# Products of an FFN block summed in any order and far behind the hidden layer, and a second attention transposed by VectorE in 32x32 squares

## The chip, the cores and the metric

The program runs on one core of one Trainium2 chip. Its time is the device time of one launch in microseconds; before the change it is 1913.87 us, the median of three runs (1910.66 to 1913.94).

Five engines work side by side, each through its own instructions in a fixed order: TensorE (PE in the profile; its weight loads stand apart as PEld), VectorE (DVE), ScalarE (ACT), GpSimd (POOL) and SyncE (SP). SP and POOL issue the transfers here. An instruction waits for the semaphores of those it needs, and all that stands behind it on its engine waits with it.

## The reference

Two parts follow each other: an attention through 32 inducing points (the matrix `inducing`, 32x128) on four batches of 12480 rows of 128, and then a feed-forward layer with a squared ReLU on all 49920 rows.

```python
def mab(q, kv):
    s = scale * (q @ kv.transpose(0, 2, 1))
    s = s - s.max(-1, keepdims=True)
    a = np.exp(s)
    a /= a.sum(-1, keepdims=True) + 1e-09
    return a @ kv
h = mab(I, x)                       # 32 x 128 for each batch
x = mab(x, h).reshape(B * S, D)     # 49920 x 128
h = np.maximum(x @ w_in, 0.0)       # 49920 x 2048
out = (h * h) @ w_out               # 49920 x 128
```

## The kernel before

**Units.** A batch is cut into 13 units of 960 rows, so there are 52 units. The *first attention* (class `First`, the inducing points ask all rows) of the units of the next batch runs beside the main work, one unit for each unit; the *second attention* (class `Second`, the rows ask the 32 results) of the next unit likewise. At the end of a batch's first attention, `first_end` joins the sums, and multiplies the joined result with `w_in` once per batch (tile `hw`). So the hidden layer of a unit is one product of the second attention's weights (tile `st`) with `hw`.

**An FFN block** (`ffn_block`) is half a unit, 480 rows. It has four *quads* of four slices of 128 hidden columns. For each quad: two pairs of products `h <- st, hw` (line 782), each pair into one of two PSUM buffers; a Relu by ACT for each pair into one of four tiles `g` (line 790); one Square by ACT for the quad (line 801); a rounded copy `hi` (line 808 by DVE for quads 0 and 2, line 806 by a casting transfer that POOL issues for quads 1 and 3; three buffers); the rest `lo = g - hi` by DVE (line 812; two buffers); and twelve products into the output sum `op` (line 825): four of `hi` with `wo_hi`, four of `hi` with `wo_lo`, four of `lo` with `wo_hi`. They are added to the plan in pairs, and each pair needs the pair before it (`last`), so within a block they stand in one fixed order. The block's sum is transposed by DVE (`rows`, line 840) and stored by four transfers of SP (line 844).

**The second attention** of a unit: scores in four groups of 32 partitions (line 626, `na <- xt, hT`); a copy out of PSUM by DVE (`ss`); two transposes by PE (line 644, `s2t`); maximum, subtraction, Exp by ACT (line 658), sum, reciprocal and share (lines 651 to 672); split into a rounded part and the rest (`sk`, lines 676 and 680); four products with the identity that turn it back (line 687, `ap`); a copy out by ACT or DVE (`sw`); and four transfers of SP (line 702) that spread it into `st`, where each half unit has the weights of its 480 rows in four bands of 32 partitions.

**What sets the order.** `Plan` is a list scheduler that runs before the program is emitted. Each task has an engine, a duration in ns, needs, buffers and a due time. Of the tasks that can start on an engine (within 40 ns of its being free) the one with the earliest due time goes first. The plan's order is the order of the instructions on each engine. Units are due every `PERIOD` = 32000 ns; a block's products are due 8000 ns after its quad's hidden layer, the second attention from `NARROW` = 6000 ns after the unit's start. `narrow` puts the second attention's scores, the first attention's scores (line 430) and its sums (line 484, `nb`) into one task; that task needs `begun`, the first hidden product of the unit that runs.

Of the kernel before, what the change touches and what calls it, by code (L numbers as in the profile page):

```python
# [154 lines left out]
def induced_attention_then_squared_relu_ffn(  # L155
# [17 lines left out]
    NQ = NF // 4  # L173
    GB, HB, LB = 4, 3, 2
# [31 lines left out]
    identr = const.tile([P, P], F32R, name="identr")  # L206
    nc.vector.tensor_copy(identr, ident)

# [408 lines left out]
    class Second:  # L617
# [6 lines left out]
        def score(self, where):  # L624
            for q in range(Q):
                nc.tensor.matmul(  # L626
                    where[q * M:(q + 1) * M, :].rearrange("m (k t) -> m k t", k=2), self.s["hT"][:, :M],
                    self.s["xt"][self.u].rearrange("c (k q t) -> c q k t", k=2, q=Q)[:, q],
                    start=True, stop=True,
                )  # L630

        def weigh(self, scored, where, bank_, due, step):
            v = {}
            n, s, u = self.n, self.s, self.u
            G = 2 * Q

            def evict():
                v["ss"] = att.tile([P, 2 * TS], F32, tag="ss", name=f"ss_{n}")
                copy(te, v["ss"], where())

            def turn():
                v["tp"] = tp = bank(f"s2t_{n}")
                for k in range(2):
                    nc.tensor.transpose(  # L644
                        tp[:TS, k * P:(k + 1) * P], v["ss"][:, k * TS:(k + 1) * TS], ident
                    )

            def top():
                v["tv"] = v["tp"][:TS, :2 * P].rearrange("t (g m) -> t g m", m=M)
                v["mx"] = tiny.tile([TS, G, 1], F32, tag="mx2", name=f"mx2_{n}")  # L650
                nc.vector.tensor_reduce(v["mx"], v["tv"], axis=AX.X, op=ALU.max)  # L651

            def sub():
                v["d"] = att.tile([TS, G, M], F32, tag="d", name=f"d_{n}")
                nc.vector.tensor_sub(v["d"], v["tv"], v["mx"].broadcast_to([TS, G, M]))  # L655

# [3 lines left out]
            def total():  # L660
                v["z"] = tiny.tile([TS, G, 1], F32, tag="z2", name=f"z2_{n}")
                nc.vector.tensor_reduce(v["z"], v["d"], axis=AX.X, op=ALU.add)  # L662
# [4 lines left out]
            def invert():  # L667
                v["rz"] = tiny.tile([TS, G, 1], F32, tag="rz2", name=f"rz2_{n}")
                nc.vector.reciprocal(v["rz"], v["z"])

            def share():
                nc.vector.tensor_mul(v["d"], v["d"], v["rz"].broadcast_to([TS, G, M]))

            def high():
                v["sk"] = att.tile([TS, Q, 2, 2, M], F32R, tag="sk", name=f"sk_{n}", bufs=1)
                nc.vector.tensor_copy(v["sk"][:, :, :, 0, :], v["d"].rearrange("t (k q) m -> t q k m", q=Q))

            def low():
                sk = v["sk"]
                nc.vector.tensor_sub(  # L680
                    sk[:, :, :, 1, :], v["d"].rearrange("t (k q) m -> t q k m", q=Q), sk[:, :, :, 0, :]
                )

            def back():
                v["ap"] = ap = bank(f"ap_{n}")
                for q in range(Q):
                    nc.tensor.matmul(  # L687
                        ap[:, q * TS:(q + 1) * TS],
                        v["sk"][:, q].rearrange("t k a m -> t (k a m)"),
                        identr[:TS, :TS], start=(q == 0), stop=(q == Q - 1), skip_group_check=True,  # L690
                    )

            def stacked():

                v["sw"] = att.tile([P, BLK], F32R, tag="sw", name=f"sw_{n}")
                copy(ts, v["sw"], v["ap"][:, :BLK])

            def spread():
                st = att.tile([P, 2, BLK], F32R, tag="st", name=f"st_{n}")
                for k in range(2):  # L700
                    for j in range(2):
                        nc.sync.dma_start(
                            st[j * 64:(j + 1) * 64, k, :].bitcast(F32),
                            v["sw"][k * 64:(k + 1) * 64, :].bitcast(F32),
                        )
                s["st", u] = st

            bt, ba, bw = Buffer("m"), Buffer("m"), Buffer("sw")
# [4 lines left out]
            t = add("DVE", 340, top, d + step, [t], reads=[bt])  # L713
            td = add("DVE", 340, sub, d + step, [t], reads=[bt])
# [5 lines left out]
            th = add("DVE", 210, high, d + 4 * step, [t], port=True)  # L720
            tl = add("DVE", 335, low, d + 5 * step, [th], port=True)
# [4 lines left out]
    def narrow(second, f, g, due, step, begun=None):  # L726
# [4 lines left out]
        needs = [begun]  # L731
# [7 lines left out]
        def go():  # L739
            if bank_a:  # L740
                v["a"] = bank(f"na_{second.n if second else f.n}")
            if second:
                second.score(v["a"][:, :2 * TS])
            if f:
                f.score(v["a"][:, 2 * TS:4 * TS])
# [7 lines left out]
        if f:  # L753
            f.weigh(t, lambda: v["a"][:, 2 * TS:4 * TS], bank_a, due)
# [168 lines left out]
```

## Time and profile before

| | |
|---|---|
| median of three runs | 1913.87 us |
| the profiled execution's own time | 1910.1 us |
| its span, first to last instruction | 1908.3 us |
| mean granted clock of TensorE | 0.986 of full speed |
| PE busy | 1710.5 us (90%) |
| ACT busy | 1590.1 us (83%) |
| DVE busy | 1462.8 us (77%) |
| POOL busy | 128.9 us (7%) |

Matmuls overlap each other: the mean of one (390 ns) is its latency, and eight in a row take far less than eight times that. So a busy PE is no measure of the work it has left; how often weight loads start in an unbroken row tells more. The names of tiles are the program's without their numbers; `h` and `op` are the two halves of the feed-forward layer.

### The profile page before, as it was taken

The numbers are of one execution on the slowest core, as the hardware profiler recorded it, in microseconds if no ns is written. First come the engines' busy times: TensorE is split into PE (matmuls) and PEld (weight loads), VectorE is DVE, ScalarE is ACT, GpSimd is POOL, SyncE is SP. The second block draws the span as 40 slices with busy tenths as digits, with TensorE's granted clock in tenths as the row PEclk, the third lists the DMA queues.
The fourth block names the chain that finished last, engine by engine and source line by source line (L and its number), as shares of the span: only waits on it lengthen the run. The fifth ranks groups of instructions, "written<-read, shape, count | busy, mean of one in ns | idle before, by whom it ended". The sixth has DMA issues, their size and how long they took to land.

```text
span 1908.3 us, 24030 instructions
## 1 busy us (share of the span) xinstructions
PE 1710.5 (90%) x8897; PEld 1342.1 (70%) x8897; DVE 1462.8 (77%) x1548; ACT 1590.1 (83%) x1602; POOL 128.9 (7%) x230
## 2 busy tenths in 40 slices
PE   7698989889998998989998989899999999998997
PEld 4377767777777777777777767777777777776776
DVE  6677777777887777878787778777777877777776
ACT  5578888788888888888888888888888888888886
POOL 1200000000000000000000000000000000000000
PEclk9799999999999999999999999999999999999999
DMA  9656756666666757667747657667444544444453
GB/s 216 121 156 159 179 159 164 174 159 165 168 165 165 177 163 179 162 173 167 190 141 171 157 170 184 163 164 178 145 140 130 161 148 153 134 152 147 141 159 120
DMA packets 458736, 306.12 MB, mean 160 GB/s; under 512 B 366172, under 2 KB 431484, under 8 KB 458620
## 3 DMA queue, kind: packets, MB, share of 16 engines
q1 hardware_dynamic: 428668, 100.11, 30.7%
q0 software_dynamic: 29952, 204.49, 29.6%
q8 instruction: 70, 1.15, 0.3%
q14 instruction: 46, 0.38, 0.1%
HBM read 48.94 MB, written 25.56 MB: 39 GB/s over the span
## 4 chain that ended last, share of the span: by engine, by line
PE 37%; ACT 21%; issue 15%; DVE 14%; DMA 11%; SPq 2%; DVEq 0%; ACTq 0%; POOLq 0%; POOL 0%
PE op L825 27%; ACT g L790 12%; DVE lo L812 7%; ACT g L801 7%; PE h L782 7%; DMA hi<-g 6%; DVE hi L808 3%; DMA xq<-in_x_dram 3%; SPq L397 1%; DMA words_i<-in_moe_w_in_dram 1%; DVE xt L401 1%; PE wp L586 1%; PE na L626 1%; DVE d L655 1%; ACT d L658 1%
## 5 line engine op out<-in xcount | busy, mean ns | idle before, releaser
L790 ACT ACTIVATE g<-h 128x960 f32<-128x960 f32 x832 | 769.5, 970 | 178.1 <-PE h L782 171.3
L812 DVE TENSOR_TENSOR lo<-g,hi 128x1920 fp32r<-128x1920 f32 x416 | 882.4, 2153 | 36.9 <-DMA hi<-g 28.8
L801 ACT ACTIVATE g<-g 128x1920 f32<-128x1920 f32 x416 | 752.7, 1809 | 5.7
L782 PE MATMUL h<-st,hw 128*128 128x480 f32 x1664 | 481.7, 393 | 104.3 <-ACT g L790 100.0
L825 PE MATMUL op<-hi,wo_hi 128*128 128x480 f32 x1664 | 452.4, 392 | 27.4 <-DMA hi<-g 25.3
L825 PE MATMUL op<-lo,wo_hi 128*128 128x480 f32 x1664 | 429.5, 385 | 17.9 <-DVE lo L812 17.5
L782 PEld LDWEIGHTS h<-st,hw 128*128 128x128 f32 x1664 | 298.4, 189 | 201.1 <-ACT g L790 159.0
L825 PE MATMUL op<-hi,wo_lo 128*128 128x480 f32 x1664 | 429.6, 383 | 0.0
L808 DVE CAST hi<-g 128x1920 fp32r<-128x1920 f32 x208 | 240.8, 1158 | 227.5 <-ACT g L801 226.1
L825 PEld LDWEIGHTS op<-hi,wo_hi 128*128 128x128 f32 x1664 | 303.6, 190 | 103.4 <-DMA hi<-g 41.7
L825 PEld LDWEIGHTS op<-lo,wo_hi 128*128 128x128 f32 x1664 | 305.7, 188 | 81.9 <-DVE lo L812 37.3
L825 PEld LDWEIGHTS op<-hi,wo_lo 128*128 128x128 f32 x1664 | 315.9, 190 | 51.6 <-issue 1.4
L806 POOL DMA_DIRECT2D hi<-g x208 | 110.6, 532 | 1701.6 <-ACT g L801 1366.3
L840 DVE STREAM_TRANSPOSE rows<-op 128x480 f32<-128x480 f32 x104 | 70.7, 679 | 82.6 <-PE op L825 82.6
L658 ACT ACTIVATE d<-d 120x256 f32<-120x256 f32 x52 | 21.7, 417 | 55.4 <-DVE d L655 55.4
L687 PEld LDWEIGHTS ap<-identr,sk 120*128 120x128 f32 x208 | 28.3, 190 | 37.5 <-DVE sk L680 30.6
L687 PE MATMUL ap<-identr,sk 120*128 120x120 f32 x208 | 32.6, 279 | 21.5 <-DVE sk L680 21.2
L401 DVE STREAM_TRANSPOSE xt<-xq 128x960 f32<-128x960 f32 x39 | 45.8, 1174 | 3.9 <-PE na L626 3.8
L651 DVE TENSOR_REDUCE mx<-s2t 120x8 f32<-120x256 f32 x52 | 21.8, 419 | 20.2 <-PE s2t L644 20.0
L662 DVE TENSOR_REDUCE z<-d 120x8 f32<-120x256 f32 x52 | 20.8, 401 | 17.0 <-ACT d L658 17.0
L235 ACT COPY et<-ep 120x256 f32<-120x256 f32 x52 | 19.4, 374 | 16.7 <-PE ep L464 16.0
L626 PE MATMUL na<-xt,hT 128*32 128x240 f32 x416 | 32.7, 387 | 0.0
(91 smaller groups left out, 611.1 us busy)
## 6 DMA issues: line engine op xcount, KB each, us to landing
hi<-g POOLq DMA_DIRECT2D x208, 960.0 KB, 4.1
xn<-in_x_dram SPq DMA_DIRECT2D x52, 480.0 KB, 5.2
st<-sw SPq DMA_DIRECT2D x208, 120.0 KB, 2.3
out_dram<-rows SPq DMA_DIRECT2D x416, 60.0 KB, 2.0
xq<-in_x_dram SPq DMA_DIRECT2D x156, 120.0 KB, 4.4
words_i<-in_moe_w_in_dram SPq DMA_DIRECT2D x4, 512.0 KB, 9.2
words_o<-in_moe_w_out_dram SPq DMA_DIRECT2D x4, 512.0 KB, 7.5
ind_sb<-in_inducing_dram SPq DMA_DIRECT2D x1, 16.0 KB, 1.7
```

What stands on the lines that cost most here:

```text
L401: nc.vector.transpose(self.xt, v["xq"].rearrange("p g c -> p (g c)"))
L626: nc.tensor.matmul(where[q * M:(q + 1) * M, :].rearrange("m (k t) -> m k t", k=2), self.s["hT"][:, :M], self.s["xt"][self.u].rearrange("c ...
L658: nc.scalar.activation(v["d"], v["d"], AF.Exp, scale=scale)
L687: nc.tensor.matmul(ap[:, q * TS:(q + 1) * TS], v["sk"][:, q].rearrange("t k a m -> t (k a m)"), identr[:TS, :TS], start=(q == 0), stop=(q ...
L782: nc.tensor.matmul(c["hp"][:, l, :BLK], s["hw"][:, f * P:(f + 1) * P], s["st", u][:, k, :], start=True, stop=True,)
L790: nc.scalar.activation(v["g"][:, 2 * i:2 * i + 2, :], c["hp"][:, :, :BLK], AF.Relu)
L801: nc.scalar.activation(v["g"], v["g"], AF.Square)
L806: nc.gpsimd.dma_start(v["hi"], v["g"])
L808: nc.vector.tensor_copy(v["hi"], v["g"])
L812: nc.vector.tensor_sub(v["lo"], v["g"], v["hi"])
L825: nc.tensor.matmul(w["op"][:, :BLK], wo[:, 4 * j + l, :], v[name][:, l, :], start=(j == m == l == 0), stop=(j == NQ - 1 and m == 2 and l = ...
L840: nc.vector.transpose(w["rows"].rearrange("p g c -> p (g c)"), w["op"][:, :BLK])
```

## The change

The products of a block no longer form a chain: each pair needs only its input and the block's first pair, so the plan may put them in any order, and they are due 18000 ns after their quad instead of 8000. The scores of a unit's second attention no longer need `begun`, but the spread (`ready`) of the unit two before. In the second attention, the scores are laid out so that each group of 32 partitions holds 240 rows of the unit and 16 more that belong to another group (width 256, a multiple of 32); DVE transposes 32x32 squares straight out of PSUM, the softmax runs as before on 128 partitions, DVE transposes back, splits in two, and sixteen transfers of 32 partitions by 240 columns spread it. The two PE transposes, the four turning products, their two PSUM banks and both copies out of PSUM are gone.

```diff
+    LANE, WIDE = UNIT // Q, 256
+    LANES = [[(0, q * LANE, WIDE)] for q in range(Q - 1)] + [[(0, UNIT - LANE, LANE), (LANE, 0, WIDE - LANE)]]
...
         def score(self, where):
             for q in range(Q):
-                nc.tensor.matmul(
-                    where[q * M:(q + 1) * M, :].rearrange("m (k t) -> m k t", k=2), self.s["hT"][:, :M],
-                    self.s["xt"][self.u].rearrange("c (k q t) -> c q k t", k=2, q=Q)[:, q],
-                    start=True, stop=True,
-                )
+                for to, from_, n in LANES[q]:
+                    nc.tensor.matmul(
+                        where[q * M:(q + 1) * M, to:to + n], self.s["hT"][:, :M],
+                        self.s["xt"][self.u][:, from_:from_ + n], start=True, stop=True,
+                    )
...
             def turn():
-                v["tp"] = tp = bank(f"s2t_{n}")
...
+                v["d"] = tile_of("d")
+                nc.vector.transpose(v["d"].rearrange("p g m -> p (g m)"), where())
...
+            def back():
+                v["a"] = tile_of("a")
+                nc.vector.transpose(v["a"].rearrange("p g m -> p (g m)"), v["d"].rearrange("p g m -> p (g m)"))
...
             def spread():
                 st = att.tile([P, 2, BLK], F32R, tag="st", name=f"st_{n}")
-                for k in range(2):
+                flat = st.rearrange("p k t -> p (k t)")
+                for q in range(Q):
                     for j in range(2):
-                        nc.sync.dma_start(
-                            st[j * 64:(j + 1) * 64, k, :].bitcast(F32),
-                            v["sw"][k * 64:(k + 1) * 64, :].bitcast(F32),
-                        )
+                        for a in range(2):
+                            nc.sync.dma_start(
+                                flat[(2 * j + a) * M:(2 * j + a + 1) * M, q * LANE:(q + 1) * LANE].bitcast(F32),
+                                v["sw"][q * M:(q + 1) * M, a, :LANE].bitcast(F32),
+                            )
...
-            te = add("DVE", 317, evict, d, [scored], reads=[bank_])
-            t = add("PE", 150, turn, d + step, [te], takes=[bt])
...
+            t = add("DVE", 335, turn, d, [scored], reads=[bank_])
...
-            t = add("PE", 460, back, d + 5 * step, [tl], takes=[ba])
-            ts = add(ST, (455, 565), stacked, d + 6 * step, [t], takes=[bw], reads=[ba])
-            self.ready = add("SP", 1000, spread, d + 7 * step, [ts], takes=[self.bst], reads=[bw])
+            t = add("DVE", 335, back, d + 4 * step, [t])
+            th = add("DVE", 210, high, d + 5 * step, [t], port=True, takes=[bw])
+            tl = add("DVE", 340, low, d + 5 * step, [th], port=True, reads=[bw])
+            self.ready = add("SP", 7000, spread, d + 6 * step, [tl], takes=[self.bst], reads=[bw])
...
-                                start=(j == m == l == 0), stop=(j == NQ - 1 and m == 2 and l == 3),
+                                start=len(done) == 1, stop=len(done) == 3 * NF,
...
-                    last = add("PE", 438, products, due + 8000 + 600 * (2 * m + i), [from_, last, w_outs[j]],
-                               takes=[bo] if begin else [], reads=[buf] + ([] if begin else [bo]))
+                    sums.append(add(
+                        "PE", 438, products, due + 18000 + 600 * (2 * m + i), [from_, w_outs[j]] + sums[:1],
+                        takes=[bo] if begin else [], reads=[buf] + ([] if begin else [bo]),
+                    ))
...
-        t = add("DVE", 570, rows, end + 1500, [last], reads=[bo], late=LATE_OT, takes=[br])
+        t = add("DVE", 570, rows, end + 1500, sums, reads=[bo], late=LATE_OT, takes=[br])
...
+        before = seconds[w - 1].ready if w else None
...
-            narrow(seconds[w + 1], f, g, t_u + NARROW, STEP, begun)
+            narrow(seconds[w + 1], f, g, t_u + NARROW, STEP, before)
```

The order on PE where the first block of unit 8 of the second batch begins, before (`h_8_0_1` is the second pair of that block, `op_7_1` the sum of the block before it, `hi_7_1_2` that block's third quad):

```order
L782 MATMUL h_8_0_0_7211<-st_8_7106,hw_4569 128x480 x2
L626 MATMUL na_9_7214<-xt_9_3067,hT_4567 32x240 x4
L430 MATMUL na_9_7214<-xt_9_6974,indT 32x240 x4
L484 MATMUL nb_8_7223<-xn_8_6345,et_8_7040 32x128 x8
L825 MATMUL op_7_1_7157<-hi_7_1_1_7179,wo_hi 128x480 x4
L825 MATMUL op_7_1_7157<-hi_7_1_1_7179,wo_lo 128x480 x4
L782 MATMUL h_8_0_1_7251<-st_8_7106,hw_4569 128x480 x2
L782 MATMUL h_8_0_2_7254<-st_8_7106,hw_4569 128x480 x2
L825 MATMUL op_7_1_7157<-lo_7_1_1_7243,wo_hi 128x480 x4
L825 MATMUL op_7_1_7157<-hi_7_1_2_7208,wo_hi 128x480 x4
L825 MATMUL op_7_1_7157<-hi_7_1_2_7208,wo_lo 128x480 x4
L825 MATMUL op_7_1_7157<-lo_7_1_2_7232,wo_hi 128x480 x4
```

The same place after the change:

```order
L764 MATMUL h_8_0_0_7360<-st_8_7247,hw_4625 128x480 x2
L764 MATMUL h_8_0_1_7363<-st_8_7247,hw_4625 128x480 x2
L807 MATMUL op_7_1_7310<-hi_7_1_1_7291,wo_lo 128x480 x2
L807 MATMUL op_7_1_7310<-lo_7_1_1_7344,wo_hi 128x480 x2
L764 MATMUL h_8_0_2_7375<-st_8_7247,hw_4625 128x480 x2
L807 MATMUL op_7_1_7310<-lo_7_1_1_7344,wo_hi 128x480 x2
L807 MATMUL op_7_1_7310<-hi_7_1_2_7334,wo_hi 128x480 x2
L764 MATMUL h_8_0_3_7386<-st_8_7247,hw_4625 128x480 x2
L807 MATMUL op_7_1_7310<-hi_7_1_2_7334,wo_hi 128x480 x2
L764 MATMUL h_8_0_4_7395<-st_8_7247,hw_4625 128x480 x2
L807 MATMUL op_7_1_7310<-hi_7_1_2_7334,wo_lo 128x480 x4
L807 MATMUL op_7_1_7310<-lo_7_1_2_7365,wo_hi 128x480 x4
```

Between `h_8_0_0` and `h_8_0_3` before there are 24 products of the sum in groups of four, and `h_8_0_3` stands behind all of quad 2; after, there are 8 between `h_8_0_0` and `h_8_0_3`, in groups of two between single pairs of `h`, and `h_8_0_4` stands ahead of eight of quad 2's twelve.

The second attention of unit 8 on DVE, before, from the maximum (`mx_1_8`, read from the PSUM bank `s2t_8` that PE has transposed) to the split (`sk_8`); `hi`, `lo` and `rows` are the feed-forward layer's:

```order
L651 TENSOR_REDUCE mx_1_8_7029<-s2t_8_7006 120x8
L812 TENSOR_TENSOR lo_7_0_0_7034<-g_7_0_0_6936,hi_7_0_0_7001 128x1920
L655 TENSOR_TENSOR d_8_7050<-s2t_8_7006,mx_1_8_7029 120x256
L840 STREAM_TRANSPOSE rows_6_1_7052<-op_6_1_6859 128x480
L662 TENSOR_REDUCE z_1_8_7061<-d_8_7050 120x8
L665 TENSOR_SCALAR z_1_8_7061<-z_1_8_7061 120x8
L669 RECIPROCAL rz_1_8_7076<-z_1_8_7061 120x8
L672 TENSOR_TENSOR d_8_7050<-d_8_7050,rz_1_8_7076 120x256
L676 CAST sk_8_7080<-d_8_7050 120x8x32
L680 TENSOR_TENSOR sk_8_7080<-d_8_7050,sk_8_7080 120x8x32
L808 CAST hi_7_0_2_7085<-g_7_0_2_7019 128x1920
```

After the change, from the sum's safe form (`z_1_8`) to the split (`sw_8`); `a_8` is the second transpose, and the first one (`d_8<-na_8`) stands where the copy `ss_8` stood, behind the scores:

```order
L657 TENSOR_SCALAR z_1_8_7142<-z_1_8_7142 128x8
L661 RECIPROCAL rz_1_8_7158<-z_1_8_7142 128x8
L789 CAST hi_7_0_2_7162<-g_7_0_2_7097 128x1920
L664 TENSOR_TENSOR d_8_7045<-d_8_7045,rz_1_8_7158 128x256
L793 TENSOR_TENSOR lo_7_0_2_7192<-g_7_0_2_7097,hi_7_0_2_7162 128x1920
L793 TENSOR_TENSOR lo_7_0_1_7204<-g_7_0_1_7047,hi_7_0_1_7121 128x1920
L668 STREAM_TRANSPOSE a_8_7216<-d_8_7045 128x256
L442 TENSOR_REDUCE mx_9_7222<-na_9_7172 128x1
L672 CAST sw_8_7226<-a_8_7216 128x256
L789 CAST hi_7_1_0_7228<-g_7_1_0_7166 128x1920
L675 TENSOR_TENSOR sw_8_7226<-a_8_7216,sw_8_7226 128x256
```

PE is no longer asked between the scores and the split. Before, `sk_8` was split while unit 7's first block ran and was then turned back by PE; now the second transpose stands between share and split, four instructions of the feed-forward layer stand inside the chain, and the first attention's maximum for unit 9 (`mx_9`) is there before unit 8's split has ended.

SP's queue around unit 8's spread, before:

```order
L380 DMA xn_10_6941<-in_x_dram 120x8x128
L397 DMA xq_10_6983<-in_x_dram 32x30x32 x4
L844 DMA out_dram<-rows_6_1_7052 32x15x32 x4
L702 DMA st_8_7106<-sw_8_7099 64x480 x4
L844 DMA out_dram<-rows_7_0_7196 32x15x32 x4
```

After:

```order
L396 DMA xq_10_7073<-in_x_dram 32x30x32 x4
L827 DMA out_dram<-rows_6_1_7146 32x15x32 x4
L379 DMA xn_11_7196<-in_x_dram 120x8x128
L685 DMA st_8_7247<-sw_8_7226 32x240 x16
L396 DMA xq_11_7329<-in_x_dram 32x30x32 x4
L827 DMA out_dram<-rows_7_0_7325 32x15x32 x4
```

The spread has sixteen issues for four, and stands right behind a load of 960 rows (`xn_11`) where it stood behind stores.

## Rows read from the trace of the kernel before

**Rows 1.** The page: busy time of each engine, and what the chain of waits was made of.
```profile
PE 1710.5 (90%) x8897; PEld 1342.1 (70%) x8897; DVE 1462.8 (77%) x1548; ACT 1590.1 (83%) x1602; POOL 128.9 (7%) x230
PE 37%; ACT 21%; issue 15%; DVE 14%; DMA 11%; SPq 2%; DVEq 0%; ACTq 0%; POOLq 0%; POOL 0%
```

**Rows 2.** The timeline at the ends of three blocks: start, duration, what DVE does (the transpose of a block's finished sum), and its wait. They are the first block of unit 0, of unit 38 and of unit 51.
```profile
108.81 0.68 DVE L840 STREAM_TRANSPOSE rows<-op 128x480 f32<-128x480 f32 x1 [2.69 <-PE op L825]
...
1457.42 0.68 DVE L840 STREAM_TRANSPOSE rows<-op 128x480 f32<-128x480 f32 x1 [0.54 <-PE op L825]
...
1890.01 0.68 DVE L840 STREAM_TRANSPOSE rows<-op 128x480 f32<-128x480 f32 x1 [2.62 <-PE op L825]
```

**Rows 3.** Busy time in two stretches of one unit each (bounds, length, then busy us and instructions of PE, PEld, DVE, ACT, POOL, the granted clock, the DMA share, GB/s). The last lies in the fourth batch, where no first attention runs beside the main work.
```profile
890.60:925.50 34.90, 31.79 (x169) 25.23 (x168) 27.36 (x29) 30.14 (x31) 2.12 (x4) 1.00 0.65 168
...
1553.90:1586.90 33.00, 30.47 (x143) 24.38 (x142) 25.75 (x25) 28.71 (x26) 2.12 (x4) 1.00 0.48 154
```

**Rows 4.** Who waited for whom over the whole span: engine and what it was to do, the releaser, total us, times, the longest.
```profile
DVE hi L808 <- ACT g L801: 226.1, 171, 3.7
ACT g L790 <- PE h L782: 171.3, 172, 2.9
PEld h L782 <- ACT g L790: 159.0, 180, 2.6
DVE rows L840 <- PE op L825: 82.6, 56, 2.7
...
PEld op L825 <- DMA hi<-g: 41.7, 43, 3.7
PEld op L825 <- DVE lo L812: 37.3, 56, 1.2
...
PEld ap L687 <- DVE sk L680: 30.6, 33, 1.2
DVE lo L812 <- DMA hi<-g: 28.8, 28, 3.4
...
PEld op L825 <- DVE hi L808: 7.2, 16, 0.8
```

**Rows 5.** Weight loads in the timeline (start, duration): where a group starts right behind another, the difference of the starts is PE's pace.
```profile
814.97 1.72 PEld L825 LDWEIGHTS op<-hi,wo_hi 128*128 128x128 f32 x8
816.72 1.73 PEld L825 LDWEIGHTS op<-hi,wo_lo 128*128 128x128 f32 x8
...
823.68 0.16 PEld L626 LDWEIGHTS na<-xt,hT 128*32 128x32 f32 x8 [0.34 <-issue]
825.10 0.72 PEld L825 LDWEIGHTS op<-hi,wo_hi 128*128 128x128 f32 x4 [0.20 <-issue]
...
831.55 0.36 PEld L644 LDWEIGHTS s2t<-ident,ss 128*120 128x120 f32 x2
831.88 0.30 PEld L782 LDWEIGHTS h<-st,hw 128*128 128x128 f32 x2
...
840.64 0.52 PEld L687 LDWEIGHTS ap<-identr,sk 120*128 120x128 f32 x4 [0.94 <-DVE sk L680]
841.08 0.74 PEld L825 LDWEIGHTS op<-hi,wo_hi 128*128 128x128 f32 x4
...
1556.91 0.16 PEld L626 LDWEIGHTS na<-xt,hT 128*32 128x32 f32 x8 [0.34 <-issue]
1557.45 0.73 PEld L825 LDWEIGHTS op<-hi,wo_hi 128*128 128x128 f32 x4 [0.39 <-issue]
```

**Rows 6.** ACT in the timeline.
```profile
808.14 1.83 ACT L801 ACTIVATE g<-g 128x1920 f32<-128x1920 f32 x1
809.85 1.84 ACT L790 ACTIVATE g<-h 128x960 f32<-128x960 f32 x2
...
822.04 2.72 ACT L790 ACTIVATE g<-h 128x960 f32<-128x960 f32 x3
824.66 1.80 ACT L801 ACTIVATE g<-g 128x1920 f32<-128x1920 f32 x1
```

**Rows 7.** Groups of instructions (busy us in total, mean ns of one | idle before them).
```profile
L840 DVE STREAM_TRANSPOSE rows<-op 128x480 f32<-128x480 f32 x104 | 70.7, 679 | 82.6 <-PE op L825 82.6
L401 DVE STREAM_TRANSPOSE xt<-xq 128x960 f32<-128x960 f32 x39 | 45.8, 1174 | 3.9 <-PE na L626 3.8
L235 ACT CAST sw<-ap 128x480 fp32r<-128x480 f32 x39 | 21.9, 561 | 0.6 <-PE ap L687 0.4
L235 DVE COPY ss<-na 128x240 f32<-128x240 f32 x52 | 20.8, 399 | 1.5 <-PE na L626 1.5
L586 PE MATMUL wp<-w_in_sb,hT 128*128 128x512 f32 x32 | 20.5, 733 | 4.2 <-DVE hw L595 2.1 <-DVE hT L580 1.5 <-DVE ss L235 0.5
L235 DVE CAST sw<-ap 128x480 fp32r<-128x480 f32 x13 | 8.5, 657 | 14.2 <-PE ap L687 14.2
```

**Rows 8.** One line of the kernel each: min/median/max ns of one issue, and under it the time from issue to landing in us; first the spread's transfers on SP, then the casting transfers on POOL.
```profile
L702 SPq DMA_DIRECT2D st<-sw x208: 467/596/1461, 74.7 to 1852.7; - x104
...
DMA to landing us min/median/max: 2.2/2.3/5.9
...
L806 POOL DMA_DIRECT2D hi<-g x208: 530/530/730, 90.0 to 1895.4; - x104
...
DMA to landing us min/median/max: 3.9/4.1/8.4
```

More of the change, by code (lines that the diff above doesn't have):

```diff
@@ L682, in low @@
                 )
[L684 to L696, printed above, removed]
@@ L706, in spread @@
                 s["st", u] = st
-            bt, ba, bw = Buffer("m"), Buffer("m"), Buffer("sw")
+            bw = Buffer("sw")
             self.bst = Buffer("st")
             d = due
-            te = add("DVE", 317, evict, d, [scored], reads=[bank_])
-            t = add("PE", 150, turn, d + step, [te], takes=[bt])
-            t = add("DVE", 340, top, d + step, [t], reads=[bt])
-            td = add("DVE", 340, sub, d + step, [t], reads=[bt])
+            t = add("DVE", 335, turn, d, [scored], reads=[bank_])
@@ L715, in weigh @@
+            t = add("DVE", 320, top, d + step, [t])
+            td = add("DVE", 340, sub, d + step, [t], port=True)
             tp = add("ACT", 307, power, d + 2 * step, [td])
@@ L719, in weigh, with narrow @@
             t = add("DVE", 340, share, d + 4 * step, [t], port=True)
-            th = add("DVE", 210, high, d + 4 * step, [t], port=True)
-            tl = add("DVE", 335, low, d + 5 * step, [th], port=True)
-            t = add("PE", 460, back, d + 5 * step, [tl], takes=[ba])
-            ts = add(ST, (455, 565), stacked, d + 6 * step, [t], takes=[bw], reads=[ba])
-            self.ready = add("SP", 1000, spread, d + 7 * step, [ts], takes=[self.bst], reads=[bw])
-    def narrow(second, f, g, due, step, begun=None):
+            t = add("DVE", 335, back, d + 4 * step, [t])
+            th = add("DVE", 210, high, d + 5 * step, [t], port=True, takes=[bw])
+            tl = add("DVE", 340, low, d + 5 * step, [th], port=True, reads=[bw])
+            self.ready = add("SP", 7000, spread, d + 6 * step, [tl], takes=[self.bst], reads=[bw])
+    def narrow(second, f, g, due, step, before=None):
         v = {}
@@ L730, in narrow @@
         bank_b = Buffer("m") if g else None
-        needs = [begun]
+        needs = [before]
         if second:
@@ L742, in go @@
             if second:
-                second.score(v["a"][:, :2 * TS])
+                second.score(v["a"][:, :WIDE])
             if f:
-                f.score(v["a"][:, 2 * TS:4 * TS])
+                f.score(v["a"][:, WIDE:WIDE + 2 * TS])
             if g:
@@ L753, in narrow @@
         if f:
-            f.weigh(t, lambda: v["a"][:, 2 * TS:4 * TS], bank_a, due)
+            f.weigh(t, lambda: v["a"][:, WIDE:WIDE + 2 * TS], bank_a, due)
         if second:
-            second.weigh(t, lambda: v["a"][:, :2 * TS], bank_a, due, step)
+            second.weigh(t, lambda: v["a"][:, :WIDE], bank_a, due, step)
         if g:
@@ L766, in ffn_block, with quad @@
         part = PERIOD / 2 / NQ
-        last = None
-        def quad(j, last):
+        sums, done = [], []
+        def quad(j):
             v = {}
@@ L871, in induced_attention_then_squared_relu_ffn @@
         t_u = t_main + w * PERIOD
-        begun = [ffn_block(b, u, k, seconds[w], t_u + k * PERIOD / 2, [opened] if w == 0 else []) for k in range(2)][0]
+        for k in range(2):
+            ffn_block(b, u, k, seconds[w], t_u + k * PERIOD / 2, [opened] if w == 0 else [])
         nxt = units[w + 1] if w + 1 < len(units) else None
```

47 lines of the change are left out of this document (17 added, 30 removed).

## The prediction

> **What bounds the kernel now.** I read the page first: PE is busy 90% of the span, ACT 83%, DVE 77%, and the chain of waits changes engine all the time, with no line that owns it [rows 1]. So the question is what PE's 90% hides. A unit of 960 rows takes, from the ends of the blocks of units 0, 38 and 51, (1457.42 - 108.81) / 38 = 35.49 us while the first attention runs beside it, and (1890.01 - 1457.42) / 13 = 33.28 us in the last batch without it [rows 2]. In an unbroken row eight weight loads take 816.72 - 814.97 = 1.75 us, 0.219 us for each matmul [rows 5]. The 128 products of a unit are 28.0 us of that pace. By the same starts, scores and sums of both attentions (`na`, `nb`) take 1.42 us, the two transposes `s2t` 0.33, the two of `ep` in the first attention are taken as equal, 0.33, and `ap` 0.44 [rows 5]: 30.5 us of work. `hw` adds 20.5 us / 4 = 5.1 per batch [rows 7], three times in 38 units, 0.4 each. So PE loses 35.49 - 30.5 - 0.4 = 4.6 us per unit. In the last batch, where `na` is 0.54 [rows 5] and `ep` is missing, work is 28.0 + 0.54 + 0.33 + 0.44 = 29.3 and the loss 4.0. Weighted, 4.4 us per unit: some 225 us of the whole.
>
> The list of waits says where: weight loads of `h` wait 159.0 us for Relu to free their PSUM buffer, while ACT waits 171.3 us for `h`; those of `op` wait 41.7 for the casting transfer, 37.3 for `lo`, 7.2 for DVE's `hi`; those of `ap` 30.6 for the split [rows 4]. Of these 276 us, 58% are `h`, 11% `ap`, 31% `op`. PE and ACT wait for each other in turn, since PE stands at an `h` with nothing else placed there.
>
> **The change part by part.**
> *Products in any order, and later.* No product is added or removed. What goes is the stall at `h`: a later due time lets the plan put a pair of products between two pairs of `h`, as the order shows: 8 products between `h_8_0_0` and `h_8_0_3` in groups of two, where 24 stood in groups of four. Relu frees a buffer every 0.87 us (2.62 us for three), a Square takes 1.71 [rows 6]; a quad on ACT is two Relus and one Square, 1.75 + 1.71 = 3.46 us, and on PE 16 x 0.219 = 3.50 us. The two now run at one pace and have something to do in the other's gaps. What is late next is `lo`: DVE must deliver it at the same pace, with two buffers.
>
> *PE's part of the second attention.* `s2t` and `ap` go: 0.33 + 0.44 = 0.77 us per unit. The scores read 1024 columns for 960, at most 0.05 us more (64/960 of `na`'s share of 1.42 and one short matmul). New work of PE per unit: 30.5 - 0.77 + 0.05 = 29.8 us, in the last batch 29.3 - 0.72 = 28.6.
>
> *ACT.* The copy `sw` goes from ACT in 39 of 52 units, 21.9 us in all, 0.42 per unit [rows 7]. ACT was busy 30.1 of 34.9 us [rows 3]; 29.7 are left, as much as PE's new work.
>
> *DVE.* Out go `ss`, 0.40, and `sw`, 8.5 us / 52 = 0.16; in come two transposes of 128x256. The trace has them with 480 columns out of PSUM, 679 ns, and with 960 out of SBUF, 1174 ns [rows 7]: 1.03 ns per column more, so 0.45 us for 256 columns (an estimate from these two rows; even at the 0.68 us of 480 columns the two would cost 0.46 more). DVE pays 0.90 - 0.56 = 0.34 us per unit, 27.4 + 0.3 = 27.7 us busy [rows 3]. It hides beside PE's 29.8, with 2 us to spare where it had 7.5.
>
> *The spread.* Sixteen issues for four on SP's queue. One takes 0.596 us (0.467 to 1.461), and lands 2.3 us after it (5.9 at the most) [rows 8]. The last of four lands 3 x 0.6 + 2.3 = 4.1 us after the first issue, the eighth of sixteen (the first block's half) 6.5, the last 11.2. Who waits is the next unit's first `h`. By the new order 48 matmuls of `h` and `op` and an `ep` stand between the split of unit 8 and `h_8_0_0`, at PE's pace 10.8 us. So the first half is there 4 us early, and the second half by `h_8_1_0`. Behind it on SP stand a load and stores that nothing waits for within 10 us. I take 0; the other end, every landing at its worst of 5.9 us and the first `h` held for all sixteen, is 8.9 + 5.9 - 10.8 = 4.0 us per unit.
>
> The Trainium skill has a rule against this step: "SBUF — State Buffer", section "The DMA setup-cost knee", says that each transfer pays about 2 us whatever its size and that one should coalesce. If each paid them in turn, an estimate from that page is 12 x 2 = 24 us more, so that `h` would wait 4.1 + 24 - 10.8 = 17 us in each unit and the time be near 2620 us. The trace differs: the next transfer is issued 0.6 us after one that lands in 2.3 [rows 8], and a sum by rows charges the issues alone.
>
> *Leftover.* With no stall at all the span is 108.8 (up to the first block's end) + 38 x (29.8 + 0.4) + 13 x 28.6 + 18.3 (1908.3 - 1890.0) = 1646.5 us. Each us of stall per unit adds 51. The stall lies between 0 and today's 4.4. If `h` and `ap` went and the rest stayed, the list of waits would leave 31%, 1.4 us. But ACT (29.7) and DVE (27.7) are now close under PE, and three engines coupled by two PSUM buffers and two `lo` buffers will not mesh without a gap, so I add to it and take 2.0, near the middle: 1646.5 + 102 = 1748.5. The execution stands 1.8 us above its span, and the median 3.8 above the execution: 1754 us.
>
> **The rivals.**
> *DVE sets the pace.* `lo` has two buffers, and DVE runs in order: today it waits 226.1 us for a Square before `hi`, 4.35 per unit, and 82.6 us for a finished sum, 1.6 [rows 4]. If it keeps both waits, a unit costs 27.7 + 4.35 + 1.6 = 33.7, and 25.75 + 0.34 + 5.95 = 32.0 in the last batch [rows 3]: 108.8 + 38 x 34.1 + 13 x 32.0 + 18.3 = 1839, with the 5.6 us around it 1845. For it: its load and the 28.8 us that `lo` already waits for the transfer. Against it: the waits are for engines that now come sooner.
> The casts land in 4.1 us, 8.4 at the most [rows 8], so they are delayed seldom. The Trainium skill names a cause for more: "SBUF — State Buffer", section "Who interferes with whom", has GpSimd's writing of descriptors shut out while DVE holds the port they share, and a busier DVE would move the casts towards the 8.4. By that rule the time goes to this rival's; by the median row nothing is added.
>
> *Stalls at single `h` pairs: slower.* The order is fixed. Where it puts an `h` earlier than Relu frees its buffer, PE stands still although products are ready, and now all 16 pairs of a unit stand between products instead of in runs. Today PE's loads wait 159.0 us over 832 pairs, 0.19 each [rows 4]. The kernel is no faster once the stall is 35.49 - 0.4 - 29.8 = 5.3 us per unit (4.7 in the last batch), 0.32 us per pair. At 0.45 per pair it is 7.2: 1646.5 + 51 x 7.2 + 5.6 = 2019 us. Against it: 180 waits today come where no product is ready.
>
> *The spread comes late.* The 4.0 us of the worst end in each unit, on top of 2.0: 1754 + 204 = 1958 us. Unit 8's spread stands right behind a load on SP, which speaks for it; the 4 us of lead of its first half against.
>
> *The change moves little:* the plan filled the gaps already and the stalls only change names, and only PE's 0.72 us per unit is gained: 1913.9 - 51 x 0.72 = 1877 us.
>
> **How the numbers follow.** Forecast, stall 0.7 to 3.3 us, 1688 to 1821 us: 0.60. Below it 0.05. DVE's pace 0.14. Moves little 0.09. Stalls at `h` 0.07. Late spread 0.05. The range leaves out the two slower cases (0.12), what is below, and a part of the case at 1877: 1685 to 1875, 0.8. This kernel tells 0.2%, about 4 us, from no change. Only the two slower cases and a small part of the one that moves little end at or above today's time: faster 0.86, same 0.02, slower 0.12.
>
> **What would show it.** Units of 31.5 to 32.5 us between block ends; waits of `h` for Relu and of ACT for `h` under 80 us each; `s2t` and `ap` gone; two transposes of about 0.45 us; POOL's casts as long as now; first `h` of a unit not waiting for `st`. I am wrong about the leftover if `h` still waits above 150 us, about DVE if `op` waits for `lo` more than for anything else, about the spread if `h` waits for its transfer.

## The result and the profile after

The changed kernel takes 1700.23 us (median of four runs, 1696.98 to 1703.76) against 1913.9 (1910.66 to 1916.32): a ratio of 0.8885, 95% interval 0.8863 to 0.8907, 11.2% less. The forecast was 1754 in a range of 1685 to 1875: the direction and the range hold, the gain was 34% larger than forecast (214 us for 160).

The page of the changed kernel, busy time and chain, as in [rows 1]:

```profile
PE 1625.4 (96%) x8689; PEld 1327.9 (78%) x8689; DVE 1458.7 (86%) x1586; ACT 1548.8 (91%) x1563; POOL 128.1 (8%) x230
PE 75%; DMA 9%; ACT 7%; issue 4%; DVE 4%; SPq 1%; DVEq 0%; POOL 0%; POOLq 0%; ACTq 0%
```

The chain that ended last was 37% PE and went through every engine; now it is 75% PE, as is to be expected where one engine sets the pace and the others do not wait for each other in turn. The ends of the first blocks of units 0, 38 and 51, as in [rows 2] (the block's transpose is line 823 now):

```profile
120.69 0.68 DVE L823 STREAM_TRANSPOSE rows<-op 128x480 f32<-128x480 f32 x1
...
1301.48 0.68 DVE L823 STREAM_TRANSPOSE rows<-op 128x480 f32<-128x480 f32 x1
...
1682.51 0.68 DVE L823 STREAM_TRANSPOSE rows<-op 128x480 f32<-128x480 f32 x1
```

A unit takes (1301.48 - 120.69) / 38 = 31.07 us for 35.49, and (1682.51 - 1301.48) / 13 = 29.31 for 33.28 in the last batch. None of the three ends is preceded by a wait of DVE for PE's sum; before, all three were, two of them by over 2.6 us. The first end comes 11.9 us later than it did. The waits, as in [rows 4] (line 772 is Relu, 764 `h`, 782 Square, 789 `hi`, 793 `lo`, 807 `op`):

```profile
DVE hi L789 <- ACT g L782: 101.7, 100, 4.3
ACT g L772 <- PE h L764: 46.0, 58, 2.5
...
DVE rows L823 <- PE op L807: 29.6, 36, 2.0
PEld h L764 <- ACT g L772: 25.5, 75, 2.1
DVE lo L793 <- DMA hi<-g: 24.5, 17, 4.2
PEld op L807 <- DMA hi<-g: 21.1, 18, 3.2
DVE xt L400 <- DMA xq<-in_x_dram: 21.0, 3, 8.5
...
PEld op L807 <- DVE hi L789: 17.0, 4, 6.1
PE op L807 <- DVE hi L789: 15.2, 3, 5.7
```

`h` waits 25.5 us for Relu where it waited 159.0, and ACT waits 46.0 us for `h` where it waited 171.3. The waits for the casting transfer halved, those of `op` for `lo` have fallen out of the longest. Two rows stand out: DVE stands 21.0 us for `xq`, in three places, which is new, and the loads of `op` wait up to 6.1 us for DVE's `hi` in four, where sixteen waits of at most 0.8 us came to 7.2. They belong together. A whole unit, the unit at the first batch end and a stretch inside it, as in [rows 3]:

```profile
425.80:455.00 29.20, 29.20 (x176) 24.21 (x175) 26.69 (x33) 28.50 (x29) 2.49 (x5) 1.00 0.80 192
...
489.10:532.60 43.50, 36.71 (x210) 28.62 (x209) 32.92 (x42) 30.87 (x36) 2.12 (x4) 0.92 0.72 157
...
517.10:522.00 4.90, 4.89 (x13) 4.10 (x14) 4.22 (x2) 1.35 (x3) 0.00 (x0) 0.53 0.41 126
```

In the plain unit PE is busy 29.20 of 29.20 us. In the unit at the first batch end, 43.5 us long, it is not, and the timeline shows why (the last four lines are SP's queue):

```profile
93.59 1.18 DVE L400 STREAM_TRANSPOSE xt<-xq 128x960 f32<-128x960 f32 x1 [8.51 <-DMA xq<-in_x_dram]
...
514.50 1.18 DVE L400 STREAM_TRANSPOSE xt<-xq 128x960 f32<-128x960 f32 x1 [6.37 <-DMA xq<-in_x_dram]
...
515.90 1.15 DVE L789 CAST hi<-g 128x1920 fp32r<-128x1920 f32 x1
...
517.11 1.17 PE L807 MATMUL op<-hi,wo_hi 128*128 128x480 f32 x2 [4.90 <-DVE hi L789]
...
486.71 13.69 SPq L685 DMA_DIRECT2D st<-sw  x16
500.50 2.14 SPq L827 DMA_DIRECT2D out_dram<-rows  x4
502.73 0.46 SPq L379 DMA_DIRECT2D xn<-in_x_dram  x1
503.28 5.35 SPq L396 DMA_DIRECT2D xq<-in_x_dram  x4
```

At 514.50 DVE has waited 6.37 us, in order, for the load of a unit of the next batch; behind it stood the `hi` that PE's next product needs, and PE stood 4.90 us. The load's first issue came at 503.28, behind a spread of sixteen transfers, four stores and another load.

### The profile page after: what moved, and what is told of

Its sections match the earlier page's. It is cut to its first block, busy times and chain, and to the rows that moved or that the text cites. A ratio compares the mean times of both kernels' runs of the same rounds, so it can differ in the third digit from the quotient of the medians.

```text
span 1698.5 us, 24658 instructions
## 1 busy us (share of the span) xinstructions
PE 1625.4 (96%) x8689; PEld 1327.9 (78%) x8689; DVE 1458.7 (86%) x1586; ACT 1548.8 (91%) x1563; POOL 128.1 (8%) x230
## 4 chain that ended last, share of the span: by engine, by line
PE 75%; DMA 9%; ACT 7%; issue 4%; DVE 4%; SPq 1%; DVEq 0%; POOL 0%; POOLq 0%; ACTq 0%
PE op L807 53%; PE h L764 17%; DMA hi<-g 5%; ACT g L772 5%; ACT g L782 2%; DMA xn<-in_x_dram 2%; PE na L626 1%; DVE lo L793 1%; DMA xq<-in_x_dram 1%; PE wp L585 1%; SPq L396 1%; PE na L429 1%; PE nb L483 1%; DMA words_o<-in_moe_w_out_dram 1%; DVE hi L789 1%
## 5 line engine op out<-in xcount | busy, mean ns | idle before, releaser
L764 PE MATMUL h<-st,hw 128*128 128x480 f32 x1664 | 504.0, 388 | 12.6 <-ACT g L772 8.0
L807 PE MATMUL op<-hi,wo_hi 128*128 128x480 f32 x1664 | 466.4, 386 | 29.4 <-DVE hi L789 15.2
L807 PE MATMUL op<-hi,wo_lo 128*128 128x480 f32 x1664 | 452.8, 383 | 0.0
L807 PE MATMUL op<-lo,wo_hi 128*128 128x480 f32 x1664 | 448.1, 382 | 0.3 <-DVE lo L793 0.3
L807 PEld LDWEIGHTS op<-hi,wo_hi 128*128 128x128 f32 x1664 | 311.4, 190 | 90.7 <-DMA hi<-g 21.1
L764 PEld LDWEIGHTS h<-st,hw 128*128 128x128 f32 x1664 | 302.5, 189 | 82.6 <-ACT g L772 25.5
L789 DVE CAST hi<-g 128x1920 fp32r<-128x1920 f32 x208 | 239.4, 1151 | 109.7 <-ACT g L782 101.7
L626 PEld LDWEIGHTS na<-xt,hT 128*32 128x32 f32 x520 | 20.0, 110 | 26.1 <-issue 18.4
L626 PE MATMUL na<-xt,hT 128*32 128x256 f32 (+2 forms) x520 | 35.2, 354 | 0.0
L455 ACT ACTIVATE e<-na,neg 128x240 f32<-128x240 f32 x39 | 18.0, 461 | 18.5 <-DVE neg L448 13.1
L234 ACT COPY xt<-xtp 128x480 f32<-128x480 f32 x26 | 14.4, 558 | 16.7 <-PE xtp L414 16.7
L463 PE MATMUL ep<-ident,e 128*120 128x128 f32 x104 | 21.4, 288 | 8.3 <-ACT e L455 6.3
L429 PE MATMUL na<-xt,indT 128*32 128x240 f32 x312 | 25.2, 379 | 2.2 <-DVE xt L400 2.2
L650 ACT ACTIVATE d<-d 128x256 f32<-128x256 f32 x52 | 22.4, 430 | 5.3 <-DVE d L647 5.3
```

The source lines that it names most:

```text
L429: nc.tensor.matmul(where[q * M:(q + 1) * M, :], indT, self.xt[:, q * 2 * TS:(q + 1) * 2 * TS], start=True, stop=True,)
L626: nc.tensor.matmul(where[q * M:(q + 1) * M, to:to + n], self.s["hT"][:, :M], self.s["xt"][self.u][:, from_:from_ + n], start=True, stop=True,)
L650: nc.scalar.activation(v["d"], v["d"], AF.Exp, scale=scale)
L764: nc.tensor.matmul(c["hp"][:, l, :BLK], s["hw"][:, f * P:(f + 1) * P], s["st", u][:, k, :], start=True, stop=True,)
L789: nc.vector.tensor_copy(v["hi"], v["g"])
L807: nc.tensor.matmul(w["op"][:, :BLK], wo[:, 4 * j + l, :], v[name][:, l, :], start=len(done) == 1, stop=len(done) == 3 * NF,)
```

## The experiments

Every run is compared with the kernel before by its ratio, since the chips differ by 0.4% (before: 1905 to 1914 us). The changed kernel's ratio is 0.8885 [0.8863, 0.8907]. The diffs show the lines that matter; "..." stands for lines left out.

### Which part brings the gain

**The products alone.** The kernel before, with only the products' order and due time changed:

```diff
-                    last = add("PE", 438, products, due + 8000 + 600 * (2 * m + i), [from_, last, w_outs[j]],
-                               takes=[bo] if begin else [], reads=[buf] + ([] if begin else [bo]))
+                    sums.append(add(
+                        "PE", 438, products, due + 18000 + 600 * (2 * m + i), [from_, w_outs[j]] + sums[:1],
+                        takes=[bo] if begin else [], reads=[buf] + ([] if begin else [bo]),
+                    ))
...
```

Expected:

> The kernel before with the products alone changed (any order, due 18000 ns after their quad); the second attention stays on PE as it was. Theory A (a stock of products that need nothing fills PE beside every h): the stalls go as in the changed kernel, and what is left out is PE's 0.72 us per unit and the waits for ap and s2t (30.6 us over the whole): 1700 + 51 x 0.72 + up to 31 = 1740 to 1770 us. Theory B (PE's round trips to VectorE for the second attention held the order, and the products could not move past them): 1840 us or more.

Measured: 1718.23 us, ratio 0.902 [0.8996, 0.9045]. Better than Theory A's range; Theory B falls. The products alone bring 9.8 of the 11.2%.

**The second attention alone.** The changed kernel with the products of before (the diff above, reversed). Expected:

> The changed kernel with the products as before (one fixed order in a block, due 8000 ns after their quad); the second attention on VectorE, early, with sixteen transfers. Theory A: h still waits for Relu with nothing placed beside it, only PE's 0.72 us per unit and the waits for ap go: 1845 to 1880 us. Theory B: 1730 to 1790 us.

Measured: 1890.39 us, ratio 0.9922 [0.9891, 0.9952], above Theory A's range: 0.8%. Its waits:

```profile
ACT g L772 <- PE h L764: 235.5, 201, 7.6
DVE hi L789 <- ACT g L782: 171.6, 135, 5.1
PEld h L764 <- ACT g L772: 138.4, 179, 2.4
```

PE and ACT still wait for each other, ACT more than before (171.3). PE was rid of `s2t` and `ap`, and most of the freed time became waiting.

**The due time without the freedom, and the freedom without the due time.** Two runs of one line each:

```diff
-                        "PE", 438, products, due + 18000 + 600 * (2 * m + i), [from_, w_outs[j]] + sums[:1],
+                        "PE", 438, products, due + 18000 + 600 * (2 * m + i), [from_, w_outs[j]] + sums[-1:],
```

```diff
-                        "PE", 438, products, due + 18000 + 600 * (2 * m + i), [from_, w_outs[j]] + sums[:1],
+                        "PE", 438, products, due + 8000 + 600 * (2 * m + i), [from_, w_outs[j]] + sums[:1],
```

Expected of the first, a chain that is due late:

> The changed kernel with each pair of products again behind the pair before it in its block, but due 18000 ns after their quad. If the late due time alone makes the stock, 1695 to 1720 us. If the fixed order holds ready products of a quad behind the lo of another, 1740 to 1850 us, with op waiting for lo and for the casting transfer over 80 us.

Expected of the second, free products that are due early:

> The changed kernel with the products due 8000 ns after their quad again, in any order. If the stock is what counts (products must be late enough that h goes first), 1750 to 1850 us, with h waiting for Relu over 60 us. If freedom of the order alone does it, 1695 to 1715 us.

Measured: the late chain 1707.66 us, ratio 0.897 [0.8946, 0.8994]; free and early 1942.59 us, ratio 1.0194 [1.0167, 1.022], above both of its ranges, slower than the kernel before and than the run of the second attention alone, which differs from it by the chain only. So the late due time makes the gain, with or without the chain. With the late chain `h` hardly waits for Relu, nor ACT for `h`:

```profile
ACT g L772 <- PE h L764: 46.8, 75, 5.9
...
PEld h L764 <- ACT g L772: 35.4, 92, 2.2
```

At 18000 the free order is 0.85% faster than the chain. Other due times move the free order by as much (below), so no gain from freedom itself is shown. At 8000 freedom costs 2.7%. The waits of the early one show what it did there:

```profile
ACT g L772 <- PE h L764: 269.2, 222, 4.9
DVE hi L789 <- ACT g L782: 241.5, 154, 5.2
PEld h L764 <- ACT g L772: 156.3, 199, 2.4
...
PEld op L807 <- DMA hi<-g: 90.5, 82, 3.9
```

ACT waits longer for `h`, and PE 90.5 us for casting transfers, against 41.7 before. Why the plan makes worse use of its freedom there than of the chain was not tried further.

**How far is far.** Products due 13000 and 24000 ns after their quad. Expected:

> The changed kernel with the products due 13000 ns after their quad (before 8000, changed 18000; 8000 in any order gave 1942.6, 18000 gave 1700.2). If the gain grows with the distance, about halfway: 1780 to 1860 us. If it is a step (once the due time lies behind that of the h two or three quads on, h always goes first), 1695 to 1730 or 1920 and more.

> The same with 24000 ns. If the stock is bounded by the buffers (four g, three hi, two lo), no change: 1690 to 1712 us. If more distance gives more, under 1685; if products that come too late hold the buffers and stop ScalarE, over 1720, with ScalarE waiting for lo.

Measured: 13000 gives 1709.24 us, ratio 0.8967 [0.8929, 0.9006]; 24000 gives 1713.74, 0.8992 [0.8961, 0.9022]. The first is in the range of the step. The second is in none of its three: it is 1.2% slower than 18000, clear of the intervals, and ACT waits for `lo` 8.5 us, not more than the 12.6 of the changed kernel. From 8000 to 13000 the time falls by 12%, and beyond there are differences of 1% that follow no direction: in each run the plan lays the whole order anew. The code says where a step could come from: quads are due 4000 ns apart, so at 8000 a product ties with the `h` of two quads on, at 13000 it is later than that of three, and four tiles `g` let `h` run no more than four quads ahead. Shown is that nearly the whole gain lies between 8000 and 13000; that it comes in one step, and that the tie is its cause, is argued.

### Which engine sets the pace now

Two runs that add work of one engine without the plan knowing it, so that all else keeps its order. More of PE: the second attention's scores three times; more of DVE: two more transposes, of a tile that is not read again.

```diff
-            for q in range(Q):
+            for q in 3 * list(range(Q)):
                 for to, from_, n in LANES[q]:
```

```diff
             def high():
+                for _ in range(2):
+                    nc.vector.transpose(v["d"].rearrange("p g m -> p (g m)"), v["a"].rearrange("p g m -> p (g m)"))
```

Expected:

> The changed kernel with the second attention's scores computed three times into the same place, in the same order of all else: 10 short matmuls more per unit, about 2 x 0.45 = 0.9 us of PE. Theory A (PE sets the pace now and has no gaps to hide work): 52 x 0.9 = 47 us more, 1740 to 1750. Theory B (VectorE or ScalarE sets it, PE's share of 96% is waiting in disguise): under 15 us more.

> The changed kernel with two more transposes of 128x256 in each unit's chain on VectorE, written to a tile that is not read again: 2 x 0.44 = 0.88 us of VectorE per unit. Theory A (VectorE has room beside PE): under 15 us more, below 1715. Theory B (VectorE sets the pace): 46 us more, about 1746.

Measured: more of PE 1733.11 us, ratio 0.9085 [0.906, 0.9111], 0.020 above the changed kernel, 38 us of 1910. More of DVE 1703.63, ratio 0.8918 [0.889, 0.8945], whose interval overlaps that of the changed kernel. In the first, weight loads in one unit, from the scores to the next product:

```profile
817.05 1.09 PEld L626 LDWEIGHTS na<-xt,hT 128*32 128x32 f32 x28 [0.33 <-issue]
...
819.44 0.30 PEld L807 LDWEIGHTS op<-hi,wo_hi 128*128 128x128 f32 x2 [0.20 <-issue]
```

2.39 us for 1.45 in the changed kernel (490.85 to 492.30, below): 0.94 us more per unit, 49 in 52 units, of which 38 show in the time. In the second, the page, and the row of the added transposes:

```profile
PE 1629.8 (96%) x8689; PEld 1328.9 (78%) x8689; DVE 1495.3 (88%) x1690; ACT 1549.7 (91%) x1563; POOL 127.8 (8%) x230
...
L672 DVE STREAM_TRANSPOSE d<-a 128x256 f32<-128x256 f32 x104 | 45.9, 442 | 2.4
```

The added transposes take 45.9 us, and the page counts DVE 37 us busier (records of neighbours overlap a little). PE's work shows with about four fifths of itself (38 of 49 us, somewhat under Theory A's 47 and far above Theory B's 15). DVE's shows with 0.0033 x 1910 = 6 of 46 us, which the intervals do not tell from nothing; at their far ends it would be 16. So PE sets the pace and DVE does not, though a fifth of PE's added work still found room. No run added work to ACT, which is busy 91%: how close it stands behind PE is open.

### The early start, and the load behind the sixteen transfers

**The scores later.** The scores of the next unit again behind the first `h` of the unit that runs:

```diff
-            narrow(seconds[w + 1], f, g, t_u + NARROW, STEP, before)
+            narrow(seconds[w + 1], f, g, t_u + NARROW, STEP, begun)
...
```

> The changed kernel with the scores of a unit again behind the first h of the unit before (begun), not behind the spread of the unit two before. Theory A (the spread has 4 us of lead anyway and the early start matters little): 1690 to 1710. Theory C (the early start is what keeps the sixteen transfers out of h's way): 1730 us or more, with h waiting for st.

Measured: 1706.55 us, ratio 0.8944 [0.8919, 0.8968]. Theory A holds; `h` waits for `st` only once, 10.9 us at the start. The early start comes out 0.6% faster, no more than other orders of the plan differ. Without it the first block ends at 111.28 instead of 120.69 and the last batch runs at 28.95 us per unit for 29.31; what is lost are the 38 units between, 31.51 for 31.07. The wait of `xt` for `xq` is gone from its list, although the sixteen transfers and the single buffer are still there; in its place `xt` waits for PE's `na`, 17.6 us in sixteen places. So sixteen transfers alone do not make DVE stand for the load: here it took the order that the early start gives.

**Two buffers for `xq`.** With two, the load is not held until DVE has read the one before. The first try took the room from `sw`:

```diff
-    xq_pool = ctx.enter_context(tc.tile_pool(name="xq", bufs=1))
+    xq_pool = ctx.enter_context(tc.tile_pool(name="xq", bufs=2))
...
-                v["sw"] = att.tile([P, 2, WIDE], F32R, tag="sw", name=f"sw_{n}")
+                v["sw"] = att.tile([P, 2, WIDE], F32R, tag="sw", name=f"sw_{n}", bufs=1)
```

> The changed kernel with two buffers for the loaded tile xq instead of one (and one for sw instead of two, to fit). Theory A (at the start and at two batch ends VectorE stands 21 us for xq, because its load queues behind the sixteen transfers on SP, and PE and ScalarE run dry behind it): that wait under 5 us, units at the batch ends 4 to 6 us shorter, 1683 to 1693 us. Rival (the batch ends are long because of their work alone): 1696 to 1704.

Measured: 1744.02 us, ratio 0.9135 [0.91, 0.9169], slower than the changed kernel and outside both ranges. The wait for `xq` was gone, but another stood in DVE's list:

```profile
DVE sw L672 <- DMA st<-sw: 53.4, 10, 6.6
```

With one `sw`, the next split waits until the sixteen transfers have read it, and DVE stands in order as it had stood for `xq`. The mistake was in the edit, and it prices the spread: ten meetings of DVE with it cost more than all three of `xq`. The second try leaves `sw` at two and takes the room from `a` and `e1`:

> The changed kernel with two buffers for xq, and the room taken from the tiles a and e1 (one buffer each) instead of sw, whose single buffer made VectorE wait 53.4 us for the spread's transfers in the run before. Theory A (VectorE's stand for xq behind the sixteen transfers is what makes the start and two batch ends long): the wait for xq under 5 us, first block's end at 116 or sooner, the two units of 43.5 us at 37 to 38 with no loss behind them, 1680 to 1692 us. Rival (the time only moves into the next unit): 1696 to 1704.

Measured: 1685.85 us, ratio 0.8855 [0.8825, 0.8886]; the profiled span is 1683.7 us against 1698.5. The wait of `xt` for `xq` is not in the list any more. The first block ends at 113.67 for 120.69; the two units of 43.5 us take 37.4 and 37.2. That is 7.0 + 6.1 + 6.4 = 19.5 us at the places named. But the two units behind the first batch end became 3.7 and 5.8 us longer (32.3 for 28.6 and 36.2 for 30.4), in the second of them behind a casting transfer that came late:

```profile
578.72 1.97 PE L807 MATMUL op<-hi,wo_hi 128*128 128x480 f32 x4 [4.15 <-DMA hi<-g]
```

Behind the second batch end 0.7 and 1.7 us went back. So at the first batch end the rival is right, all that was won there and more moved into the next units; at the start and the second batch end Theory A is, and 7.0 - 3.4 + 4.0 = 7.6 us are left. The other 7 of the 14.8 us between the spans came in small steps in units that never waited for `xq`, and on the chip of this run the kernel before was faster too (1906.0 us for 1913.9). By the ratios the gain is 0.0030, 6 us of 1910, and their intervals overlap: that the second buffer makes the kernel faster is not shown by the time, only that the wait is gone.

**The spread as two tasks.** With `xq` still at two buffers, eight transfers for the first block and eight for the second, each block's `h` behind its own half:

```diff
-            self.ready = add("SP", 7000, spread, d + 6 * step, [tl], takes=[self.bst], reads=[bw])
+            first = add("SP", 4700, lambda: spread(0), d + 6 * step, [tl], takes=[self.bst], reads=[bw])
+            self.ready = add("SP", 4700, lambda: spread(1), d + 9 * step, [tl, first], reads=[bw, self.bst])
+            self.half = [first, self.ready]
...
-                need = [second.ready, s["wide"][j]]
+                need = [second.half[k], s["wide"][j]]
```

> The kernel of the run before (two buffers for xq) with the spread as two tasks of eight transfers, so that loads and stores can stand between them on SP and a block needs only its own half. Theory A (little is left: PE's work of about 30.2 us in a unit of 30.9, the start and the batch ends): 1672 to 1690 us, with PE at 96% or more. Rival (the sixteen transfers on SP still cost at each unit): under 1668. If a half that comes late costs more than the queue gains: over 1695, with h waiting for st.

Measured: 1687.97 us, ratio 0.8837 [0.8804, 0.8869]: no difference from the run before it. Theory A holds, with PE at 96%. The two have the lowest ratios of this study, though both intervals still touch that of the changed kernel.

## Why the prediction was right, and which terms were off

*What bounds it.* The reading that PE lost 4.4 us per unit, most of it at `h`, was right, and so was the cure: with products placed between pairs of `h` its waits for Relu fell from 159.0 to 25.5 us, and the products alone bring 9.8 of the 11.2%. It works as the prediction has it, "a later due time lets the plan put a pair of products between two pairs of `h`"; the free order that came with it shows no gain of its own.

*PE's work* was put at 29.8 us and 28.6 in the last batch. Scores and sums take 1.45 us against an expected 1.47 (below). The unit from 425.80 to 455.00 us, which PE fills wholly, takes 29.2, but it is only a rough check: 122 of a unit's 128 products (32 of `h`, 90 of `op`) and two units' sums stand in it.

```profile
490.85 0.16 PEld L626 LDWEIGHTS na<-xt,hT 128*32 128x32 f32 x8 [0.34 <-issue]
...
492.30 1.16 PEld L807 LDWEIGHTS op<-hi,wo_hi 128*128 128x128 f32 x6 [0.20 <-issue]
```

*The leftover* is the term that was mis-sized: "I add to it and take 2.0, near the middle". Measured, and with the prediction's own figures for the work, it is 31.07 - 0.4 - 29.8 = 0.87 us per unit in 38, and 29.31 - 28.6 = 0.71 in 13. Two units at each of two batch ends, 34.1 and 43.5, hold most of it: without these four the other 34 average (1180.8 - 155.2) / 34 = 30.2 us, which leaves 0.4 over the work. The units came out under the 31.5 to 32.5 us that were to show the forecast right. So three engines that run within 2 us of each other did mesh but for a few tenths of a us in a plain unit. The reason given for adding to it, that DVE and ACT are close under PE, is refuted for DVE by the run with more transposes; for ACT it stays open. That the time fell inside the range is owed to the range's width, not to the middle value.

By terms the forecast span was 1748.5 and 1698.5 came: 11.9 more up to the first block's end, 38 x 1.13 = 42.9 less, 13 x 1.29 = 16.8 less, 2.3 less at the tail. The start was taken over from the kernel before, 108.8, without a reason given. It did not stay: 9.4 of the 11.9 us are gone where the scores wait for `begun` again, and 7.0 with the second `xq` buffer.

*The spread* was taken as 0, because "Behind it on SP stand a load and stores that nothing waits for within 10 us". That step failed, though what it cost is a small part of the whole. The transfers themselves are as read, 589 ns each to issue and 2.1 us to land:

```profile
L685 SPq DMA_DIRECT2D st<-sw x832: 507/589/2319, 77.1 to 1636.3; - x167
...
DMA to landing us min/median/max: 1.7/2.1/7.3
```

and `h` waits for `st` once, 4.1 us, at the start, as it did before (3.7). But the load behind them is `xq`, and DVE, which at the first batch end was ready for it 5 us after its first issue, meets it in order: 21.0 us in three places, in the order that the early start gives. PE stood behind it 15.2 us in three places; a second buffer removed the wait, and about 6 us by the ratios, within the intervals. The rule of the Trainium skill that was weighed here ("SBUF — State Buffer", section "The DMA setup-cost knee"), if each transfer paid in turn, would have had each unit wait 17 us. The trace agrees with that section's 2 us for a transfer (2.1 us to landing) and not with paying it in turn: the issues follow each other every 0.589 us.

*DVE's two transposes* cost 441 and 437 ns for the 0.45 expected:

```profile
L640 DVE STREAM_TRANSPOSE d<-na 128x256 f32<-128x256 f32 x52 | 23.0, 441 | 2.0 <-PE na L626 1.9
...
L668 DVE STREAM_TRANSPOSE a<-d 128x256 f32<-128x256 f32 x52 | 22.7, 437 | 0.6
```

*The rivals.* DVE's pace: DVE still waits 101.7 us for Squares, but not at its own cost, as the added transposes showed. The casts land in 4.6 us for 4.1, and products that stand far behind notice little (their loads wait 21.1 us in 18 places, for 41.7 in 43). That is the direction of the Trainium skill's rule in "SBUF — State Buffer", section "Who interferes with whom", though nothing here separates it from the fuller DMA queues (180 GB/s for 160). Stalls at single `h` pairs: 25.5 us over 832 pairs, 0.03 each, a tenth of the 0.32 from which it would have decided. Moves little: it is what the second attention's part does by itself, 1890 us. It was wrong to price that part at PE's whole 0.72 us per unit with PE waiting anyway; added to the late products, where PE sets the pace, it brings 0.902 - 0.8885 = 1.35%, 26 us of the 37 that 52 x 0.72 would be. Part of the difference between 0.8 and 1.35% can be the order that the plan lays anew, which alone moved the time by 1%.

## What to carry to other kernels

Where two engines wait for each other in turn, the cure is work in stock that needs nothing: here a due time that lies far behind the producer's brought nearly the whole gain, and freedom of the order without it was a loss. Ask what an engine's saved work is worth while that engine still waits: the same cut brought 0.8% with PE waiting and 1.35% with PE setting the pace, a difference near what a new order alone makes, and a price by PE's whole time was too high in both. And before a step on a queue is priced at nothing, follow what stands behind it to the engine that will meet it in its own order, at the start and at the ends of batches too.

## What the runs showed of the hardware

The granted clock fell after a stand of PE: from 511.0 to 517.1 us PE was busy 0.70 us, and in the 4.9 us that follow its clock is 0.53 of full speed, so nearly all of them at the lower of its two levels, 1.2 of 2.4 GHz; from 522.0 it is 1.00 again:

```profile
511.00:517.10 6.10, 0.70 (x2) 0.30 (x2) 2.57 (x4) 6.10 (x8) 0.53 (x1) 0.81 1.04 220
...
522.00:528.00 6.00, 6.00 (x30) 5.15 (x29) 4.79 (x4) 2.95 (x3) 0.00 (x0) 1.00 0.27 72
```

PE is busy 4.89 of those 4.9 us, so the stand at a batch end costs some 2.3 us more behind it (an estimate from these rows, 4.9 x 0.47), which the sum of the prediction had not.
